# Two transformer layers on one core: the last MLP chunk gets a structure of its own

## The chip, the core and the metric

The kernel runs on one core of a Trainium2 chip. The metric is device time in microseconds (us) from launch to end. Five engines work in parallel, each through its own instruction stream in order: PE (TensorE, matrix products; PEld is its weight load), DVE (VectorE), ACT (ScalarE), POOL (GpSimd) and SP (SyncE, which issues most of the DMAs here). They meet only through semaphores.

## The reference

The input x has 2048 tokens of 640 bf16 values. Two layers are applied, each of them an attention part A and an MLP part B ("the mixer"), with one shared set of weights:

```
x = x + A(layernorm(x));  x = x + B(layernorm(x));  x = x + A(layernorm(x));  x = x + B(layernorm(x))

A: for each of 64 segments of 32 tokens, one after the other:
     h = [8 memory tokens, 32 tokens]                 # 40 rows
     q, k, v = h Wq, h Wk, h Wv                       # 640 -> 32 heads x 192
     o = softmax(mask(q k^T / sqrt(192))) v Wo        # -> 640
     memory of the next segment = the first 8 rows of o; output = the other 32
B: h  = gelu(layernorm(x) w1)                         # 640 -> 640
   hs = (h, its four quarters of columns moved by +1, -1, +2, -2 tokens) w2
   x1 = x + hs
   y  = x1 + gelu(layernorm(x1) w3) w4                # 640 -> 1536 -> 640
```

## The kernel before

A runs as 69 steps of `attention_step`. Step t handles segment t of the first layer (lane 0) and segment t - 5 of the second layer (lane 1) side by side, so that its matrix products have 80 columns; in the first five and in the last five steps only one lane is alive and they have 40. A step walks over 8 groups of 4 heads. `proj_pair` makes the projections for two groups (L541; results leave PSUM at L551, L559, L565 and L571, and `v` is transposed at L579), and `attend` makes scores, softmax and the output projection (L606 to L670, sum in `psy`). Most of the weights don't fit in SBUF: they are streamed again in every step through a ring of 8 slots (`wst`, L453).

B runs in chunks of 64 tokens per lane. `chunk` and `chunk_end` of number c are spread over the attention steps that follow, as filling for PE. A normal chunk does this, in order: transposes of the attention output back to rows (`psx`, L836), the residual sum (L847), layer norm statistics (`ln_ops`: two BN_STATS at L707, aggregation at L708, then variance + eps as two columns at L713 and L715, and the power -1/2 for both on POOL at L721), the normalised rows (L727), transposes (`psv`, L735), a copy of the result to SBUF by ACT (L896), w1 (`psh`, L918), `gelu` (ACT square L752, DVE L756, ACT tanh L760, DVE L765), w2 (`hs`, L963), the sum at L969, a second layer norm, transposes, copy (L983), w3 (L998), gelu, w4 (`y`, L1024), the sum at L1030 and the stores (L1042). Because w2 needs tokens beyond the chunk, a look-ahead is carried along for four rows: transposes `psl` (L843), a sum (L851), statistics (L874 to L876, POOL at L881), normalised rows (L887), which are written to the same buffer `vbg` as those of L727, a second set of transposes and a second copy (L900). After a normal chunk a third layer norm makes the input of the second layer's attention (`psn`).

The last chunk, `chunk(NCH - 1)`, has no attention step left to hide in. It starts when the last step's output is in `yTB` (L696), and everything in it follows in series. Its tokens are the last 34 and the last 64 before them. After the gelu of w1, seven small copies (`fc2`, L947) join its two lanes. Its w2, w3 and w4 are cut by the arrival of the weight loads, not by columns.

At the start, buffers are cleared by POOL (L373, L376, L380) and DVE ahead of everything else in their queues; POOL then issues three loads and computes the power of the first layer norm (L721), on which the first rows for attention wait (L727). Meanwhile SP loads the weights.

No order is written by hand. Each operation is given an estimated duration and a due time; `Plan.place` simulates the engines with these and fixes the order of all instructions before the program is built. A load that the plan holds back (`paced`) gets a wait on the PE operation that ends last before its planned start. A change of an estimated duration can thus move instructions elsewhere.

Of the kernel before, what the change touches and what calls it, by code (L numbers as in the profile page):

```python
# [29 lines left out]
OT_BUFS = 8  # L30
LAT = 0.12
# [44 lines left out]
class Plan:  # L76
# [47 lines left out]
    def place(self):  # L124
# [27 lines left out]
        def est(o, t):  # L152
            s = max(t, o.ready)
            need = {}
            for b in o.slots:
                if b.slot is None:
                    need[b.cls] = need.get(b.cls, 0) + 1
            for c, n in need.items():
                fs = self.free_slots[c]
                if len(fs) < n:  # L160
                    return None
                s = max(s, fs[n - 1][0])
            if o.e == "SP":
                s = max(s, srv - ahead(o))
            return s
# [6 lines left out]
        while left:  # L172
# [29 lines left out]
            o.paced = e == "SP" and s <= srv - ahead(o) + 1e-9  # L202
# [38 lines left out]
def kernel(  # L241
# [87 lines left out]
    mask_b = ctile([L1, L1], bf16, "mask_b")  # L329
    nc.gpsimd.memset(mask_b[:], 0.0)  # L330
    keep(mask_b, L1, M, L1, -M, 1, -1, NEG)
    keep(mask_b, L1, M, L1, -M, 1, 0, 0.0)
# [11 lines left out]
    qT = qTw[:].rearrange("p (c n) -> p c n", c=GC)  # L344
    vFw = ctile([P, GC * NS], bf16, "vF")
    vF = vFw[:].rearrange("p (c n) -> p c n", c=GC)
    kT = [ctile([P, 8, NS], bf16, f"kT{i}") for i in range(2)]
    Vt = [ctile([NS, 2 * VP], bf16, f"V{i}") for i in range(2)]
# [23 lines left out]
    for i in range(2):  # L372
        nc.gpsimd.memset(kT[i][:], 0.0)  # L373
    for i in range(2):
        nc.vector.memset(Vt[i][:], 0.0)
    nc.gpsimd.memset(yTB[:], 0.0)  # L376
    nc.vector.memset(qTw[:], 0.0)
    nc.vector.memset(vFw[:], 0.0)
    nc.vector.memset(Pmw[:], 0.0)
# [131 lines left out]
    def attention_step(t):  # L511
# [4 lines left out]
        maskt = mask2[:] if both else (mask_a if 0 in ln else mask_b[:])  # L516
# [8 lines left out]
        def proj_pair(pr):  # L525
            s0 = base + sl * 2 * pr
            for kind, off in (("k", 0.0), ("q", 0.2), ("v", 0.5)):
                wbs, wv = load_pair(kind, pr, s0 + off * 2 * sl, LEAD_A)
                for j in range(2):
                    g = 2 * pr + j  # L530
                    G = t * NG + g
                    due = s0 + (off + 0.1 * j) * 2 * sl
# [3 lines left out]
                    for kcs in [range(0, nres)] + [range(kc, kc + 1) for kc in range(nres, KC)]:  # L536
                        def fn(op, pq=pq, wv=wv, j=j, kcs=kcs):
                            o = T(pq)
                            for cc in range(GC):
                                for kc in kcs:  # L540
                                    nc.tensor.matmul(out=o[:, cc, 0:N],  # L541
                                                     lhsT=wv(kc, GW * j + cc * P, GW * j + (cc + 1) * P),
                                                     rhs=h[:, kc, c0:c0 + N], start=(kc == 0 and cc == 0),
                                                     stop=(kc == KC - 1), skip_group_check=True)
                        wb = wbs[0] if kcs[0] == 0 else wbs[1 + kcs[0] - nres]
                        add("PE", mm_us(N, k=GC * len(kcs)), due + 0.01 * kcs[0], fn, r=(wb, *hk), a=(pq,))
                    if kind == "q":
                        q = qT

                        def fq(op, pq=pq, q=q):  # L550
                            nc.scalar.copy(out=q[:, :, 0:N], in_=T(pq)[:, :, 0:N])  # L551
                        add("ACT", act_us(GC * N), due, fq, r=(pq,), w=(B("qT"),))
                    elif kind == "k":
                        k_ = kT[G % 2]

                        def fk(op, pq=pq, k_=k_):
                            p4 = T(pq)[:].rearrange("p (h c) n -> p h c n", h=2)
                            k4 = k_[:].rearrange("p (h c) n -> p h c n", h=2)
                            nc.vector.tensor_copy(out=k4[:, :, 0::3, 0:N], in_=p4[:, :, 0::2, 0:N])  # L559
                        add("DVE", dve_us(4 * N), due, fk, r=(pq,), w=(B("kT", G % 2, 0),))  # L560
                        for part, (r0, r1, jj) in enumerate(((0, 64, 1), (64, P, 2))):
                            def fk2(op, pq=pq, k_=k_, r0=r0, r1=r1, jj=jj):
                                p4 = T(pq)[:].rearrange("p (h c) n -> p h c n", h=2)
                                k4 = k_[:].rearrange("p (h c) n -> p h c n", h=2)
                                nc.vector.tensor_copy(out=k4[r0:r1, :, jj, 0:N], in_=p4[r0:r1, :, 1, 0:N])  # L565
                            add("DVE", dve_us(2 * N), due, fk2, r=(pq,), w=(B("kT", G % 2, 1 + part),))
                    else:
                        vf, V_ = vF, Vt[G % 2]

                        def fvf(op, pq=pq, vf=vf):  # L570
                            nc.scalar.copy(out=vf[:, :, 0:N], in_=T(pq)[:, :, 0:N])  # L571
# [3 lines left out]
                        def fvt(op, pvt=pvt, vf=vf):  # L575
# [6 lines left out]
                        for hf in range(2):  # L582
                            def fe(op, pvt=pvt, V_=V_, hf=hf):
                                src = T(pvt)[0:N, GWH * hf:GWH * (hf + 1)].rearrange("n (a b) -> n a b", a=2)
                                v0 = hf * (VP - 64)
                                dst = V_[0:N, v0:v0 + 512].rearrange("n (a b) -> n a b", a=2)[:, :, 64 * hf:64 * hf + Dh]
# [5 lines left out]
                                w=(B("V", G % 2, hf),))  # L592

        def attend(g):
            G = t * NG + g
            s0 = base + sl * g
            q, k_, V_ = qT, kT[G % 2], Vt[G % 2]
# [3 lines left out]
            def fs(op):  # L601
                o = T(pss)
                seq = [(0, 1, 0, 0), (1, 1, 2, 3), (2, 1, 3, 4), (3, 1, 5, 7), (0, 2, 1, 1), (2, 2, 4, 5)]
                for n_, (i, w_, c, j) in enumerate(seq):
                    m_ = wide(c, GC - 1)
                    nc.tensor.matmul(out=o[0:m_, i * N:(i + w_) * N].rearrange("p (a b) -> p a b", a=w_),  # L606
                                     lhsT=qTw[:, c * NS:c * NS + m_], rhs=k_[:, j:j + w_, 0:N],
                                     start=(n_ == 0), stop=(n_ == len(seq) - 1), skip_group_check=True)
            add("PE", mm_us(N, N, 4) + mm_us(2 * N, N, 2), hi - 4, fs,
                r=(B("qT"), B("kT", G % 2, 0), B("kT", G % 2, 1), B("kT", G % 2, 2)), w=(pss,))  # L610
# [4 lines left out]
            def f1(op):  # L615
                o = T(pss)[0:N, 0:HG * N].rearrange("p (a b) -> p a b", a=HG)
                nc.vector.tensor_tensor_reduce(out=o, in0=o, in1=maskt.unsqueeze(1).to_broadcast([N, HG, N]),  # L617
                                               scale=-scale, scalar=3.0e38, op0=ALU.add, op1=ALU.min,
                                               accum_out=sm_[0:N, 0:1])
            add("DVE", dve_us(HG * N) + 0.02, hi - 4, f1, r=(pss,), w=(pss, smk))  # L620

            def f2(op):
                o = T(pss)[0:N, 0:HG * N].rearrange("p (a b) -> p a b", a=HG)
                nc.scalar.activation(out=Pb[0:N, :, 0:N], in_=o, func=ACT.Exp, bias=sm_[0:N, 0:1], scale=-1.0)  # L624
            add("ACT", act_us(HG * N) + 0.09, hi - 4, f2, r=(pss, smk), w=(Pk,))

            def f3(op):
                nc.vector.tensor_reduce(out=sm_[0:N, 2:2 + HG], in_=Pb[0:N, :, 0:N], axis=AX.X, op=ALU.add)  # L628
                nc.vector.reciprocal(out=sm_[0:N, 6:6 + HG], in_=sm_[0:N, 2:2 + HG])
                nc.vector.tensor_tensor(out=Pb[0:N, :, 0:N], in0=Pb[0:N, :, 0:N],  # L630
                                        in1=sm_[0:N, 6:6 + HG].unsqueeze(2).to_broadcast([N, HG, N]), op=ALU.mult)
# [11 lines left out]
            def f5(op):  # L643
                nc.scalar.copy(out=Pt[:, :, 0:N], in_=T(pst)[0:NS, :, 0:N])  # L644
# [10 lines left out]
            add("PE", mm_us(N, k=8), hi - 3, f6, r=(B("PT"), B("V", G % 2, 0), B("V", G % 2, 1)), w=(pso,))  # L655
            o_ = oT[G % OT_BUFS]

            def f7(op):
                nc.vector.tensor_copy(out=o_[:, :, 0:N], in_=T(pso)[:, :, 0:N])  # L659
            add("DVE", dve_us(GC * N), hi - 4, f7, r=(pso,), w=(B("oT", G % OT_BUFS),))  # L660
            due = base + STEP - 1 + 0.02 * g if g >= NG - OT_BUFS + 1 else s0 + 2.0 * sl
            wb, wo = res_tile(("o", g), [P, GC, Dm], Wo_v[:, g], base + STEP - 2 + 0.02 * g)
            for hf in range(2):
                def f8(op, hf=hf):
                    o = T(psy)
                    for cc in range(3 * hf, 3 * hf + 3):
                        for m in range(KC):
                            st = first_wo[0]
                            first_wo[0] = False
                            nc.tensor.matmul(out=o[:, m, c0:c0 + N], lhsT=wo[:, cc, m * P:(m + 1) * P],  # L670
                                             rhs=o_[:, cc, 0:N], start=st, stop=True, skip_group_check=True)
                add("PE", mm_us(N, k=3 * KC), due, f8, r=(wb, B("oT", G % OT_BUFS)), a=(psy,))

# [26 lines left out]
    def ln_ops(src, rows, st, stk, srck, due, const_cols):  # L700
# [4 lines left out]
        def f1(op):  # L705
            for c in range(2):
                nc.vector.bn_stats(out=st[0:rows, 6 * c:6 * c + 6], in_=srcv[:, c, :])  # L707
            nc.vector.bn_aggr(out=st[0:rows, 12:14], in_=st[0:rows, 0:12].rearrange("p (c s) -> p c s", c=2))  # L708
            if const_cols:
                nc.vector.tensor_scalar(out=st[0:rows, 14:15], in0=st[0:rows, 13:14], scalar1=lnA[0:rows, 0:1],  # L710
                                        scalar2=lnA[0:rows, 1:2], op0=ALU.mult, op1=ALU.add)
            else:
                nc.vector.tensor_scalar(out=st[0:rows, 14:15], in0=st[0:rows, 13:14], scalar1=1.0, scalar2=EPS,  # L713
                                        op0=ALU.mult, op1=ALU.add)
                nc.vector.tensor_scalar(out=st[0:rows, 15:16], in0=st[0:rows, 13:14], scalar1=1.0 + EPS,  # L715
                                        scalar2=EPS * EPS, op0=ALU.mult, op1=ALU.add)
        add("DVE", 1.37, due, f1, r=(srck,), w=(stk,))
        n = 1 if const_cols else 2
# [106 lines left out]
    def chunk(c):  # L825
# [12 lines left out]
        psl = ps(PB, [TOK + 4, KC, P], bf16, "psl")  # L838
# [5 lines left out]
        add("PE", mm_us(128, k=KC), D(0.06), ftl, r=(B("yTB", 0), B("yTB", 1)), w=(psl,))  # L844
# [8 lines left out]
        add("DVE", 0.48, D(0.06), fl, r=(psl,), w=(B("lnx", "l"),))  # L853
# [13 lines left out]
        ln_ops(xw, XB, st1, s1k, xk, D(0.06), False)  # L867
# [10 lines left out]
        add("DVE", 1.42, D(0.07), f1, r=(B("lnx", "l"), B("lnx", "x")), w=(s2k,))  # L878
# [3 lines left out]
        add("POOL", 0.57, D(0.07), f2, w=(s2k,))  # L882
# [6 lines left out]
        add("DVE", 0.45, D(0.08), f3, r=(B("lnx", "l"), B("lnx", "x"), s2k), w=(vxk,))  # L889
        ps2 = ps(PB, [P, KC, XB], bf16, "psv")  # L890
        transposes(ps2, vb, XB, D(0.1), (vk,))
        psl2 = ps(PB, [P, KC, TOK + 4], bf16, "psvl")
        transposes(psl2, vx, TOK + 4, D(0.11), (vxk,))
# [3 lines left out]
        add("ACT", act_us(KC * XB), D(0.1), fe, r=(ps2,), w=(vTk,))  # L897
# [3 lines left out]
        add("ACT", act_us(KC * 4), D(0.11), fel, r=(psl2,), w=(B("vTl"),))  # L901
# [8 lines left out]
        for i, (a, e) in enumerate(((0, 2), (2, 4), (4, KC))):  # L910
# [10 lines left out]
            add("PE", mm_us(128, k=KC * (e - a)), due, fw, r=(wb, vTk, B("vTl")), a=tuple(pz))  # L921
# [5 lines left out]
        for i, (a, e) in enumerate(((0, 3), (3, KC))):  # L927
# [13 lines left out]
            gelu(pz[i], e - a, due, outs, (B("hTB", i),), own=i if last else None)  # L941
            carry += [(r, r1, n + a, o2) for (r, r1, n, _, _), o2 in zip(outs, offs)]
        if last:
            def fc2(op):
                for r, r1, n, o2 in carry:
                    if o2:
                        nc.vector.tensor_copy(out=hTB[r:r1, n, 0:o2 // 2, 0], in_=hTB[r:r1, n, TOK:TOK + o2 // 2, 1])  # L947
            add("DVE", 1.16, D(0.4), fc2, w=(B("hTB", 0), B("hTB", 1)))
# [4 lines left out]
        hs = [ps(PB, [XB, HC], f32, "hs") for _ in range(2)]  # L953
        for i, (a, e) in enumerate(((0, 2), (2, 4), (4, 5))):
            due = D(0.4 + 0.1 * i)
            wb, wv = load_b("w2", a, e, due, last=last)

# [7 lines left out]
            add("PE", mm_us(HC, k=2 * (e - a)), due, fw, r=(wb, B("hTB", 0), B("hTB", 1)), a=tuple(hs))  # L965
        for k in range(2):
# [194 lines left out]
```

## Time and profile before

| | |
|---|---|
| time, median of 3 runs | 3534.4 us (3530.97 to 3536.71) |
| the profiled execution | 3528.87 us, its span 3527.2 us |
| busy in the span | PE 94%, DVE 70%, ACT 43%, POOL 7% |
| last attention product (L670) ends | 3483.4 us |
| first product of the last chunk's w1, w2, w3 | 3491.04, 3498.50, 3506.30 us |
| last store is issued | 3517.18 us |

The span is the time from the first to the last instruction in one profiled execution; its own time is 1.7 us more. All positions are in us from the start of that span. In lists of instructions the columns are start, duration, engine, line, operation, output<-input, shapes, count and, in brackets, the idle time of the engine before it with what ended it. In tables by stretch PEclk is the clock that TensorE was granted, 1.00 being full speed.

### The profile page before, as it was taken

Reading aid. Unit: us, or ns where it says so; the run is one execution under the profiler, and the core shown is the slowest. Engines: PE = TensorE matmul, PEld = TensorE weight load, DVE = VectorE, ACT = ScalarE, POOL = GpSimd, SP = SyncE. Lnnn points to the kernel's source line nnn. Section 1 sums busy time; section 2 is a strip of 40 time slices with the busy share of each in tenths; the row PEclk is TensorE's granted clock in tenths of the full one; section 3 lists DMA queues with packets and bytes.
Section 4 is the critical chain, followed back from the end, with each engine's and each line's share of the span. In section 5 each row is a group of like instructions: output and inputs, shape, how many; then the busy total and the mean of one; then the engine's idle time right before and its main releaser. Section 6 shows DMA issues by size and latency. Waiting matters only on the chain.

```text
span 3527.2 us, 188048 instructions
## 1 busy us (share of the span) xinstructions
PE 3322.3 (94%) x84559; PEld 3231.6 (92%) x84559; DVE 2469.2 (70%) x7436; ACT 1520.6 (43%) x3569; POOL 247.1 (7%) x488
## 2 busy tenths in 40 slices
PE   5889999999999999999999999999999999999886
PEld 5879999999999999999999999999999999999775
DVE  2557777777777777777777777777777777777554
ACT  1334444444444444444444444444444444444332
POOL 0000000000000000000000000000000000000000
PEclk8899999999999999999999999999999999999897
DMA  9999898889888988898889888998889888988995
GB/s 374 304 306 317 301 324 298 294 297 316 301 307 299 315 300 299 309 321 303 302 301 327 306 295 298 316 310 303 312 305 319 298 299 301 319 300 303 307 315 176
DMA packets 497753, 1075.27 MB, mean 305 GB/s; under 512 B 49455, under 2 KB 216893, under 8 KB 496945
## 3 DMA queue, kind: packets, MB, share of 16 engines
q1 hardware_dynamic: 489712, 1050.11, 86.2%
q8 instruction: 661, 10.83, 1.2%
q0 software_dynamic: 7232, 13.13, 1.1%
q14 instruction: 148, 1.20, 0.1%
HBM read 1057.79 MB, written 5.24 MB: 301 GB/s over the span
## 4 chain that ended last, share of the span: by engine, by line
PE 88%; DMA 5%; issue 4%; DVE 1%; ACT 1%; SPq 1%; POOL 0%; POOLq 0%; DVEq 0%; ACTq 0%
PE psy L670 16%; PE psq L541 15%; PE psv L541 15%; PE psk L541 15%; PE pvt L579 5%; PE pso L653 4%; PE pss L606 4%; PE psh L998 3%; PE y L1024 3%; PE pst L639 2%; DMA wst<-in_A_Wq_dram 2%; PE psh L918 1%; DMA wst<-in_A_Wk_dram 1%; PE hs L963 1%; DMA wst<-in_A_Wv_dram 1%
## 5 line engine op out<-in xcount | busy, mean ns | idle before, releaser
L541 PEld LDWEIGHTS <-wst 128*128 128x128 bf16 x25668 | 1031.2, 100 | 43.1 <-issue 25.0
L670 PE MATMUL psy<-oT,wo 128*128 128x80 bf16 (+1 forms) x16560 | 689.8, 199 | 32.1 <-issue 19.4
L670 PEld LDWEIGHTS <-wo 128*128 128x128 bf16 x16560 | 626.3, 100 | 41.0 <-issue 29.2
L551 ACT CAST qT<-psq 128x480 bf16<-128x480 f32 (+1 forms) x552 | 292.6, 530 | 639.9 <-PE psq L541 638.6
L541 PE MATMUL psq<-hT,wst 128*128 128x80 bf16 (+1 forms) x9936 | 467.9, 199 | 19.1 <-issue 11.1
L659 DVE CAST oT<-pso 128x480 bf16<-128x480 f32 (+1 forms) x552 | 341.2, 618 | 167.2 <-PE pso L653 161.6
L541 PE MATMUL psv<-hT,wv 128*128 128x80 bf16 (+1 forms) x9936 | 434.6, 199 | 21.1 <-issue 15.9
L541 PE MATMUL psk<-hT,wst 128*128 128x80 bf16 (+1 forms) x9108 | 428.0, 199 | 11.0 <-issue 7.9
L541 PEld LDWEIGHTS <-wv 128*128 128x128 bf16 x9936 | 386.6, 100 | 28.9 <-issue 18.3
L644 ACT COPY PT<-pst 80x320 bf16<-80x320 bf16 (+1 forms) x552 | 221.9, 402 | 440.2 <-PE pst L639 433.8
L590 ACT COPY V<-pvt 80x384 bf16<-80x384 bf16 (+1 forms) x552 | 261.7, 474 | 328.5 <-PE pvt L579 301.1
L541 PE MATMUL psk<-hT,wk 128*128 128x80 bf16 (+1 forms) x7452 | 348.8, 199 | 19.5 <-ACT hT L688 10.8
L565 DVE CAST kT<-psk 64x160 bf16<-64x160 f32 (+1 forms) x1104 | 336.7, 305 | 9.7
L624 ACT ACTIVATE Pm<-pss,sm 80x320 bf16<-80x320 f32 (+1 forms) x552 | 279.7, 507 | 135.9 <-DVE sm L617 135.8
L571 ACT CAST vF<-psv 128x480 bf16<-128x480 f32 (+1 forms) x552 | 290.0, 525 | 102.0 <-PE psv L541 95.7
L541 PE MATMUL psq<-hT,wq 128*128 128x80 bf16 (+1 forms) x6624 | 320.2, 199 | 11.7 <-issue 6.6
L541 PE MATMUL psv<-hT,wst 128*128 128x80 bf16 (+1 forms) x6624 | 322.4, 199 | 7.7 <-issue 6.6
L541 PEld LDWEIGHTS <-wk 128*128 128x128 bf16 x7452 | 299.2, 100 | 26.8 <-issue 26.1
L588 DVE COPY V<-pvt 80x384 bf16<-80x384 bf16 (+1 forms) x552 | 188.1, 350 | 182.3 <-PE pvt L579 107.8
L617 DVE CUSTOM_DVE_ANT_1 pss<-pss,mask 80x320 f32<-80x320 f32 (+1 forms) x512 | 240.9, 485 | 104.7 <-PE pss L606 84.3
L559 DVE CAST kT<-psk 128x320 bf16<-128x320 f32 (+1 forms) x552 | 254.6, 461 | 69.6 <-PE psk L541 63.2
L628 DVE TENSOR_REDUCE sm<-Pm 80x4 f32<-80x320 bf16 (+1 forms) x552 | 248.9, 451 | 57.3 <-ACT Pm L624 52.2
(130 smaller groups left out, 4425.0 us busy)
## 6 DMA issues: line engine op xcount, KB each, us to landing
wst<-in_A_Wq_dram SPq DMA_DIRECT2D x828, 384.0 KB, 5.3
wst<-in_A_Wk_dram SPq DMA_DIRECT2D x759, 384.0 KB, 5.3
wst<-in_A_Wv_dram SPq DMA_DIRECT2D x552, 384.0 KB, 5.4
wstB<-in_B_w_dram SPq DMA_DIRECT2D x495, 320.0 KB, 5.0
wstB<-in_B_w_dram SPq DMA_DIRECT2D x132, 160.0 KB, 4.9
wo<-in_A_Wo_dram SPq DMA_DIRECT2D x8, 960.0 KB, 12.8
wv<-in_A_Wv_dram SPq DMA_DIRECT2D x4, 1152.0 KB, 11.9
wq<-in_A_Wq_dram SPq DMA_DIRECT2D x4, 768.0 KB, 11.7
```

The source lines that it names most:

```text
L541: nc.tensor.matmul(out=o[:, cc, 0:N], lhsT=wv(kc, GW * j + cc * P, GW * j + (cc + 1) * P), rhs=h[:, kc, c0:c0 + N], start=(kc == 0 and cc ...
L551: nc.scalar.copy(out=q[:, :, 0:N], in_=T(pq)[:, :, 0:N])
L559: nc.vector.tensor_copy(out=k4[:, :, 0::3, 0:N], in_=p4[:, :, 0::2, 0:N])
L565: nc.vector.tensor_copy(out=k4[r0:r1, :, jj, 0:N], in_=p4[r0:r1, :, 1, 0:N])
L571: nc.scalar.copy(out=vf[:, :, 0:N], in_=T(pq)[:, :, 0:N])
L590: nc.scalar.copy(out=dst, in_=src)
L617: nc.vector.tensor_tensor_reduce(out=o, in0=o, in1=maskt.unsqueeze(1).to_broadcast([N, HG, N]), scale=-scale, scalar=3.0e38, op0=ALU.add, ...
L624: nc.scalar.activation(out=Pb[0:N, :, 0:N], in_=o, func=ACT.Exp, bias=sm_[0:N, 0:1], scale=-1.0)
L628: nc.vector.tensor_reduce(out=sm_[0:N, 2:2 + HG], in_=Pb[0:N, :, 0:N], axis=AX.X, op=ALU.add)
L644: nc.scalar.copy(out=Pt[:, :, 0:N], in_=T(pst)[0:NS, :, 0:N])
L659: nc.vector.tensor_copy(out=o_[:, :, 0:N], in_=T(pso)[:, :, 0:N])
L670: nc.tensor.matmul(out=o[:, m, c0:c0 + N], lhsT=wo[:, cc, m * P:(m + 1) * P], rhs=o_[:, cc, 0:N], start=st, stop=True, skip_group_check=True)
```

## The change

In the last chunk:

- The look-ahead (`psl`, its sum, statistics, power, normalised rows, transposes, copy) is left out. The columns it filled are set to zero by a POOL memset or taken from the chunk's own transposes.
- The copy out of the transposes is cut in two, columns 0 to 2 by ACT and 3 to 4 by DVE (`halves`), for the first and for the second layer norm.
- Six of the seven small copies of `fc2` go from DVE to ACT.
- w2 and w4 are issued by halves of the output columns (k = 0, 1) within groups of row blocks, and each half has its sum (and, after w2, its BN_STATS) right behind it.
- w3 is issued as four groups of three row blocks, where it was three parts of 5, 5 and 2.
- The output is stored in four pieces, by row set and column half, issued by SP and ACT; it was two pieces issued by POOL.

Elsewhere:

- `ln_ops` makes one column of variance + eps where only one is used, which removes the DVE operation of L715 and halves the POOL power's columns in 68 layer norms; its planned duration falls from 1.37 to 1.30 us.
- In steps with lane 1 alone, operands stay at columns 40 to 79 instead of being moved to 0 to 39; the mask of their own (`mask_b`) goes. With `ONE = 40` their products keep 40 columns.
- At the start, eight buffers `oT` are cleared by POOL and four `hT` by DVE.
- Tiles are allocated in another order, `oT` is tracked by halves (`HALVES` is empty, so it is still written in one piece), and `paced` is set where the DMA rate alone delays a load.

```diff
-    mask_b = ctile([L1, L1], bf16, "mask_b")
-    nc.gpsimd.memset(mask_b[:], 0.0)
-    keep(mask_b, L1, M, L1, -M, 1, -1, NEG)
-    keep(mask_b, L1, M, L1, -M, 1, 0, 0.0)
+    mask_b = mask2[:, L1:NS]
...
+    for o_ in oT:
+        nc.gpsimd.memset(o_[:], 0.0)
...
+    for i in range(4):
+        nc.vector.memset(hT[i][:], 0.0)
...
-    def ln_ops(src, rows, st, stk, srck, due, const_cols):
+    def ln_ops(src, rows, st, stk, srck, due, n, parted=False):
...
-            for c in range(2):
+            for c in () if parted else range(2):
                 nc.vector.bn_stats(out=st[0:rows, 6 * c:6 * c + 6], in_=srcv[:, c, :])
...
+            if n == 2:
                 nc.vector.tensor_scalar(out=st[0:rows, 15:16], in0=st[0:rows, 13:14], scalar1=1.0 + EPS,
                                         scalar2=EPS * EPS, op0=ALU.mult, op1=ALU.add)
-        add("DVE", 1.37, due, f1, r=(srck,), w=(stk,))
-        n = 1 if const_cols else 2
+        add("DVE", (0.5 if parted else 1.3) + 0.07 * (n - 1), due, f1, r=(srck,), w=(stk,))
...
+        def halves(pt, due, ahead=False):
+            def fa(op):
+                nc.scalar.copy(out=vT[:, 0:3, 0:XB], in_=T(pt)[:, 0:3, :])
+            add("ACT", act_us(3 * XB), due, fa, r=(pt,), w=(vTk,))
+
+            def fd(op):
+                nc.vector.tensor_copy(out=vT[:, 3:KC, 0:XB], in_=T(pt)[:, 3:KC, :])
+            add("DVE", dve_us(2 * XB), due, fd, r=(pt,), w=(B("vTd"),))
+            if ahead:
+                def fn(op):
+                    nc.scalar.copy(out=vT[:, :, XB + 1:XB + 4:2], in_=T(pt)[:, :, 0:4:2])
+                add("ACT", act_us(KC * 2), due, fn, r=(pt,), w=(B("vTn"),))
...
+        if last:
+            def fz0(op):
+                nc.gpsimd.memset(vT[:, :, XB:XB + 4:2], 0.0)
+            add("POOL", 0.3, D(0.02), fz0, w=(vTk,))
+            halves(ps2, D(0.1), True)
...
         if last:
-            def fc2(op):
-                for r, r1, n, o2 in carry:
-                    if o2:
-                        nc.vector.tensor_copy(out=hTB[r:r1, n, 0:o2 // 2, 0], in_=hTB[r:r1, n, TOK:TOK + o2 // 2, 1])
-            add("DVE", 1.16, D(0.4), fc2, w=(B("hTB", 0), B("hTB", 1)))
+            for i in range(2):
+                mine = [x for x in carry if x[3] and (x[2] < 3) == (i == 0)]
+                for e_, part in (("ACT", mine if i == 0 else []), ("DVE", [] if i == 0 else mine)):
...
+        for u, (n0, n1) in enumerate(((0, 3), (3, 5))) if last else ():
+            for k in range(2):
+                def fw(op, k=k, n0=n0, n1=n1):
+                    for n in range(n0, n1):
+                        lhsT = hTB[:, n, 0:TOK, :].rearrange("p w l -> p (w l)")
+                        nc.tensor.matmul(out=T(hs[k])[:], lhsT=lhsT, rhs=got[n][1]()[:, got[n][2], HC * k:HC * (k + 1)],
+                                         start=(n == 0), stop=(n == 4))
...
+                if last:
+                    nc.vector.bn_stats(out=st3[:, 6 * k:6 * k + 6], in_=uw[:, cs])
...
+        for u in range(4) if last else ():
+            n0 = 3 * u
+            pz2 = ps(PB, [P, 3, XB], f32, "psh2")
+
+            def fw(op, n0=n0, pz2=pz2):
+                for kc in range(KC):
+                    for n in range(n0, n0 + 3):
+                        _, wv, j, i = w3got[n, kc]
+                        nc.tensor.matmul(out=T(pz2)[:, n - n0, :], lhsT=wv()[:, j, i * P:(i + 1) * P],
+                                         rhs=vT[:, kc, 0:XB], start=(kc == 0 and n == n0), stop=(kc == KC - 1),
+                                         skip_group_check=True)
...
+        for u, (n0, n1) in enumerate(((0, 3), (3, 6), (6, 9), (9, FC))) if last else ():
+            for k in range(2):
+                def fw(op, k=k, n0=n0, n1=n1):
+                    for n in range(n0, n1):
+                        nc.tensor.matmul(out=T(y2[k])[:], lhsT=h2T[:, n, :], rhs=got[n][1]()[:, got[n][2], HC * k:HC * (k + 1)],
+                                         start=(n == 0), stop=(n == FC - 1))
...
+                def fst(op, lane=lane, b=b, w0=w0, cs=slice(HC * k, HC * (k + 1))):
+                    (nc.scalar if lane else nc.sync).dma_start(out=outd[w0:w0 + b, cs], in_=xo[lane:2 * b:2, cs])
+                add("ACT" if lane else "SP", 0.4, D(1.6), fst, r=(B("xh", k),), dma=b * HC * 2)
```

## The prediction

> **What bounds the kernel now.** The page first: who is busy, and the chain that ended last.
>
> ```profile
> PE 3322.3 (94%) x84559; PEld 3231.6 (92%) x84559; DVE 2469.2 (70%) x7436; ACT 1520.6 (43%) x3569; POOL 247.1 (7%) x488
> PE   5889999999999999999999999999999999999886
> PEclk8899999999999999999999999999999999999897
> PE 88%; DMA 5%; issue 4%; DVE 1%; ACT 1%; SPq 1%; POOL 0%; POOLq 0%; DVEq 0%; ACTq 0%
> ```
>
> PE is the bound nearly everywhere: 88% of the chain. What relieves DVE or POOL in the middle is worth little. The exception is the end, read next in stretches of 10 us.
>
> ```profile
> 3480.00:3490.00 10.00, 3.95 (x94) 3.38 (x93) 6.56 (x20) 0.76 (x2) 1.39 (x2) 0.83 1.02 335
> 3490.00:3500.00 10.00, 4.79 (x38) 3.75 (x37) 4.39 (x18) 2.36 (x6) 0.22 (x1) 0.50 0.07 24
> 3500.00:3510.00 10.00, 5.74 (x46) 4.71 (x45) 3.48 (x11) 1.46 (x3) 0.88 (x1) 0.50 0.01 2
> 3510.00:3520.00 10.00, 5.23 (x51) 3.80 (x49) 4.50 (x12) 3.08 (x8) 1.14 (x2) 0.98 0.04 13
> ```
>
> Here no engine is busy for more than two thirds (columns: PE, PEld, DVE, ACT, POOL), TensorE runs at half clock for most of it, and the DMA engines are empty: one chain of dependent steps. The timeline shows its links.
>
> ```profile
> 3484.95 0.49 DVE L851 TENSOR_TENSOR h2u<-psl,h2u 4x640 bf16<-4x640 bf16 x1
> ...
> 3488.97 0.44 DVE L887 TENSOR_SCALAR vbg<-h2u,st 68x640 bf16<-68x640 bf16 x1
> ...
> 3489.47 0.71 PE L735 MATMUL psv<-ident,vbg 128*128 128x128 bf16 x5 [4.79 <-DVE vbg L887]
> 3490.22 0.69 ACT L896 COPY hTB<-psv 128x640 bf16<-128x640 bf16 x1 [8.93 <-PE psv L735]
> 3490.80 0.18 ACT L900 COPY hTB<-psvl 128x20 bf16<-128x20 bf16 x1
> 3491.04 2.29 PE L918 MATMUL psh<-hTB,wk 128*128 128x128 bf16 x20 [0.57 <-ACT hTB L900]
> ...
> 3495.42 2.90 DVE L765 SCALAR_TENSOR_TENSOR hTB<-wv,psh 128x128 bf16<-128x128 f32 x9 [0.33 <-ACT wv L760]
> 3498.23 1.16 DVE L947 COPY hTB<-hTB 128x3 bf16<-128x3 bf16 x7
> ...
> 3501.09 0.89 DVE L969 SCALAR_TENSOR_TENSOR h2u<-hs,h2u 128x320 bf16<-128x320 f32 x2 [1.70 <-PE hs L963]
> ...
> 3516.60 1.14 POOL L1042 DMA_DIRECT2D out_dram<-vbg  x2 [12.37 <-DVE vbg L1030]
> ```
>
> The look-ahead sits on the chain: its sum (L851) stands ahead of the main statistics on DVE, and the main transposes wait for its normalised rows (L887), since both write `vbg`.
>
> **The change part by part.** The end, from the first `psx` transpose at 3483.95.
>
> *To the first w1 product: before 3491.04, so 7.09.* After, with these rows' durations and 0.03 to 0.05 per hand-over: `psx` 0.48, sum 0.49, two BN_STATS 0.89, aggregation 0.21, the two columns 0.21, which brings POOL's power to 2.46; 0.71 (it stays at two columns) to 3.17; normalised rows 0.44 to 3.64; `psv` 0.71 to 4.40. Then the halves. They are not parallel: in the built program DVE's copy waits on the ACT semaphore at the value that ACT's copy raises, and the small ACT copy waits for DVE's. So 0.48 (ACT, 384 columns; L590 takes 0.474 for as many) + 0.30 (DVE, 256; L588 takes 0.350 for 384) + 0.18 (L900) + hand-overs = 1.1, where L896 and L900 took 0.85. First w1 product at 5.5: **-1.6**. Parallel halves would make it -1.9. The POOL memset of the padding stands far ahead in POOL's queue and costs nothing.
>
> TensorE's clock decides the 0.71 and the w1 products. The row: PEclk was 0.80 over 3486 to 3487 and 0.50 from then on, so it fell 2.1 us after the last product at 3484.7. The Trainium skill ("TensorE: Matmul & The Clock Gate", "What's actually happening") says the clock halves after at least one idle window of about 3.4 us. The gap before `psv` shrinks to about 3.2 us, so by the page alone the clock could hold through `psv` and w1: 0.3 off the transposes and about 1.2 off the 25 w1 products (2.84 at half clock), 1.5 more gain. The trace shows the fall inside such a gap; I take half clock, and keep 1.5 for the range.
>
> *w1 to the first L765:* unchanged, 4.38.
>
> *L765 to the first w3 product: before 3495.42 to 3506.30, 10.88.* The nine L765 pieces keep 2.90. Six of the seven copies run on ACT, each behind its DVE piece, at about 0.2 (L900: 0.182); the sixth ends 2.0 after the start. Products of the first three row blocks begin at once after that: ten products of 320 columns took 2.83 here, 0.27 each at half clock. Left column half to 2.3, right one to 3.15; the last DVE copy (0.17) ends at 3.1; two products more for the left half, and its sum starts at 3.8, where before it was 5.67: -1.87. The right half's last products run beside it. Sum, BN_STATS, sum, BN_STATS, aggregation now alternate with waits between: 2.10, before 1.93, +0.17. One column less, -0.07. Power (0.88 beside L976), rows and transposes stay. w3 needs only ACT's 384 columns for its first nine products (0.107 apart), and DVE's part is ready by then: -0.21. Together **-2.0**; first w3 product at 18.8, before 22.35.
>
> *w3 to the last sum: before 3506.30 to 3516.31, 10.0.* The 60 products cost the same 5.5, half of them cold. After the fourth group ACT and DVE alternate in the planned order: square to 6.0, DVE 0.55 for each of the last three steps (L756 and L765 at 384 columns), tanh 0.52; the last L765 ends at 7.8. The third group's six w4 products end at 8.2, the last six at 9.0 (0.136 each at full clock), sums at 9.15 and 9.63: **-0.4**. With cold w4 products it would be +0.9.
>
> *Stores:* the last issue began 0.87 after the last sum, behind POOL's first; now 0.1 after, on a queue of its own: **-0.8**. From issue to landing both stores took 1.9. The memory load that SP issues at 1.27 on an idle queue is used at 3.17, 1.9 as well, so I take nothing more. The skill ("DMA: Bandwidth & Descriptors", "Specifications") gives first-byte times of about 1 us from GpSimd and 0.6 from SP or ACT, an estimate of -0.4 more.
>
> End: -1.6 - 2.0 - 0.4 - 0.8 = **-4.8**.
>
> *The start.* POOL clears eight `oT` of 480 columns ahead of its loads and of the first power; `kT` with 640 took 0.62, so 0.47 each, 3.7, less 0.5 for the mask. The power moves from 7.04 to about 10.3, and PE's first projections with it.
>
> ```profile
> 7.04 0.76 POOL L721 TENSOR_TENSOR st<-st,neghalf 128x2 f32<-128x2 f32 x1
> 7.84 0.45 DVE L727 TENSOR_SCALAR vbg<-vbg,st 128x640 bf16<-128x640 bf16 x1 [3.02 <-POOL st L721]
> ...
> 12.63 0.98 PE L541 MATMUL psq<-hT,wq 128*128 128x40 bf16 x24 [1.04 <-DMA wq<-in_A_Wq_dram]
> ...
> 19.40 1.38 PE L541 MATMUL psv<-hT,wv 128*128 128x40 bf16 x36 [1.80 <-DMA wv<-in_A_Wv_dram]
> ```
>
> But PE waits for weights at 12.63, twice at about 15 and at 19.40, 3.7 in all; that covers 3.2. SP's next load into a ring slot (12.67) may go 2 us late; loads then take 12.5 from issue to landing, a backlog that covers it. Cost 0; bounds 0 and +3.2. DVE's four `hT` memsets (under 0.26 each, the price of `qT`) end long before the power.
>
> *The middle.* 68 DVE operations go, 0.07 apart behind L713. On the chain such a one appears at few places, as here:
>
> ```profile
> 1722.19 0.06 DVE st L715
> ```
>
> Five in the whole trace: **-0.3**; if every one told, -4.7. The shorter planned duration reorders little: of 10,097 PE groups 180 stand elsewhere (steps 2 to 5, 65, 67). Of 2,492 held-back loads 216 wait for another PE group, mostly one later. PE's queue, the loads' sizes and the 40-column products are unchanged. Bounds -4.7 and +10 (see the last rival); taken -0.3.
>
> **Sum:** -5.1 on the profiled 3528.87, so 3523.8. The median of the runs stands 5.5 higher, at 3534.4; from there 3529.3.
>
> **The rivals.** *A second gain* (0.35): PE keeps its clock at the end, or DVE's relief reaches PE in the middle. -5.1 with 1.5 and 0.4 at the end, or 2.3 to 4.7 in the middle: -7.5 to -12, 3522 to 3527. For it: the ordered DVE queue puts softmax pieces behind each layer norm, 67 times. Against: the chain meets that five times. *The start is not covered* (0.05): +3.2, net -1.9, 3532.5. Against: the waits above. *The loads come later* (0.10): from step 6 on, four to five of some 76 held-back loads of every two steps wait for a PE group more, 0.15 to 0.65 us. PE's idle time put to "issue", 4% of the chain in pieces of 1 to 2 us, could be late weights. If one of them per chunk delays PE by 0.4, 32 chunks cost 12.8, net +7.7, 3542. It decides from 0.16 per chunk, where the end's gain is used up. Against: a ring of eight slots lies between.
>
> **How the numbers follow.** A measurement of this kernel tells about 0.2%, 7.1 us, from no change. The forecast (0.50) has its own range 3526 to 3532; 0.08 of it lies past -7.1. Faster: 0.08 + 0.35 = 0.43; same: 0.42 + 0.05 = 0.47; slower 0.10. Range 3520 to 3537: it takes in the second gain but its far end, and the uncovered start, and leaves out the late loads.
>
> **What would show it.** Right: no L851 to L887 counterparts after the last step; first w1 product 5.5 after `psx`, first w3 product 18.8, last store issue about 28.6 (before 33.2); the two half copies one after the other; PEclk at 0.50 before w1; PE's first projection near 12.7 but `psv` still at 19.4; the last attention product within 2 us of 3483.4. Wrong: that product moved by more than 3 us either way, or `psv` at the start later by more than 1.

## The result and the profile after

The changed kernel takes 3513.57 us (median of 6 runs, 3508.64 to 3526.6), the kernel before 3535.56 us (6 runs, 3530.97 to 3538.52). The ratio is 0.9946, with a 95% interval of 0.9926 to 0.9966: 19 us faster, between 12 and 26. The forecast was 5 us faster (3529.3 us, range 3520 to 3537), less than the 7 us that it took as the least a measurement can tell from no change.

The profiled execution of the changed kernel is its slowest run, 3526.6 us (span 3524.9), only 2.3 below that of before. So the two traces must be compared by stages. The sum of the span hides that the attention part happened to run late in this execution and that the end is far shorter. First the page, then stretches of the end (PE, PEld, DVE, ACT, POOL busy; PEclk; DMA share; GB/s).

```profile
PE 3321.0 (94%) x84549; PEld 3229.3 (92%) x84549; DVE 2466.7 (70%) x7360; ACT 1522.1 (43%) x3573; POOL 235.7 (7%) x489
PE 90%; issue 4%; DMA 3%; DVE 1%; ACT 1%; SPq 0%; POOL 0%; POOLq 0%; DVEq 0%; ACTq 0%
```

```profile
3500.00:3510.00 10.00, 4.67 (x24) 2.42 (x22) 6.08 (x19) 2.75 (x10) 0.91 (x2) 0.50 0.00 0
3510.00:3520.00 10.00, 8.76 (x89) 7.07 (x89) 4.97 (x11) 4.11 (x9) 0.03 (x1) 0.79 0.01 2
3520.00:3525.00 5.00, 0.20 (x2) 0.00 (x0) 0.73 (x2) 0.00 (x0) 0.00 (x0) 0.94 0.09 25
```

Nothing is won in busy time. The last attention output (L716, L696 of before) starts at 3492.28, where before it was 3483.46, and yet the span ends 2.3 earlier. From that output to the end of the span it was 43.7 and is 32.6: **11.1 us less**. The links of that chain, from the timeline of the changed kernel:

```profile
3493.51 0.49 DVE L864 TENSOR_TENSOR xw<-psx,xw 128x640 bf16<-128x640 bf16 x1 [0.88 <-PE psx L852]
3494.03 0.89 DVE L727 BATCH_NORM_STATS2 st<-xw 128x6 f32<-128x320 bf16 x2
...
3496.75 0.72 PE L751 MATMUL psv<-ident,vbg 128*128 128x128 bf16 x5 [3.29 <-DVE vbg L743]
...
3497.51 0.48 ACT L919 COPY hTB<-psv 128x384 bf16<-128x384 bf16 x1 [7.68 <-PE psv L751]
3498.02 0.29 DVE L923 COPY hTB<-psv 128x256 bf16<-128x256 bf16 x1 [0.96 <-ACT hTB L919]
3498.40 0.18 ACT L927 COPY hTB<-psv 128x10 bf16<-128x10 bf16 x1 [0.41 <-DVE hTB L923]
3498.63 2.29 PE L959 MATMUL psh<-hTB,wk 128*128 128x128 bf16 x20 [1.16 <-ACT hTB L927]
...
3503.02 2.69 DVE L781 SCALAR_TENSOR_TENSOR hTB<-wv,psh 128x128 bf16<-128x128 f32 x9 [0.33 <-ACT wv L776]
3503.34 1.65 ACT L992 COPY hTB<-hTB 128x3 bf16<-128x3 bf16 x6
...
3506.86 0.49 DVE L1032 SCALAR_TENSOR_TENSOR h2u<-hs,h2u 128x320 bf16<-128x320 f32 x1 [1.08 <-PE hs L1024]
...
3511.91 0.80 PE L1089 MATMUL psh<-hTB,wv 128*128 128x128 bf16 x6 [0.62 <-ACT hTB L919]
...
3519.84 0.90 DVE L1133 SCALAR_TENSOR_TENSOR vbg<-y,xw 128x320 bf16<-128x320 f32 x2 [0.81 <-PE y L1125]
3520.36 1.20 ACTq L1145 DMA_DIRECT2D out_dram<-vbg  x2
3520.39 1.39 SPq L1145 DMA_DIRECT2D out_dram<-vbg  x2
```

The look-ahead is gone: BN_STATS follows the sum, and the transposes wait for the main rows. The two half copies stand one behind the other. The small copies run on ACT beside DVE's pieces. Cut at the marks that the prediction used, the end reads as follows in all six kernels profiled (E1 to E4 are the experiments below; us):

| stretch | before | E3 | E4 | changed | E1 | E2 |
|---|---|---|---|---|---|---|
| `psx` to the first w1 product | 7.09 | 7.35 | 7.34 | 5.85 | 5.85 | 5.85 |
| w1 to the first gelu piece (L765) | 4.38 | 4.39 | 4.39 | 4.39 | 4.39 | 4.38 |
| gelu piece to the first w3 product | 10.88 | 10.46 | 10.62 | 8.89 | 8.89 | 8.90 |
| w3 to the end of the last sum | 10.01 | 9.73 | 9.73 | 8.83 | 9.73 | 8.93 |
| end of the last sum to the end of the span | 10.89 | 10.82 | 4.69 | 4.16 | 10.77 | 4.33 |

The first four rows bring 1.2, 0, 2.0 and 1.2 us. The last one brings 6.7, more than all others together, in a stretch where no engine computes. What SP waits for there tells where the time goes (columns: waiting engine and line, what it waited for: total us, times, longest). Before:

```profile
SPq L1156 <- DMA out_dram<-vbg: 29.1, 1, 29.1
SPq L1156 <- PEq L1156: 7.7, 2, 7.2
```

and in the changed kernel:

```profile
SPq L1271 <- DMA out_dram<-vbg: 1.6, 2, 1.0
SPq L1271 <- PEq L1271: 0.7, 2, 0.5
```

At the end of the program SP first waits until every DMA has landed, and then meets the other engines. Before, the stores had landed by 3519.1 and the meeting still took 7.2 us; now it takes 0.5. The wait is put down to PE's queue, but PE came early: its closing DRAIN (the instruction with which each engine ends its work before the meeting) was over at 3515.6. The engine that came last was POOL. These are POOL's DRAINs in before, the changed kernel, E1 and E4 (line, engine, operation, count: least, median and longest in ns, first and last start in us):

```profile
L1156 POOLq DRAIN  x3: 46/102/9346, 3517.0 to 3526.9; - x3
L1271 POOLq DRAIN  x3: 46/93/9174, 3509.3 to 3524.6; - x3
L1271 POOLq DRAIN  x3: 46/98/9259, 3514.3 to 3524.0; - x3
L1157 POOLq DRAIN  x3: 46/102/9411, 3507.5 to 3524.4; - x3
```

The first of the three is the long one. It takes 9.2 to 9.4 us in every kernel; what differs is when POOL comes to it (its record begins up to 0.9 us before POOL's last operation ends):

| | before | E1 | E3 | E4 | changed | E2 |
|---|---|---|---|---|---|---|
| POOL's last operation | store | store | store | power | power | power |
| it ends | 3517.74 | 3514.96 | 3525.91 | 3508.46 | 3510.03 | 3502.07 |
| POOL's long DRAIN ends | 3526.38 | 3523.52 | 3534.55 | 3516.96 | 3518.45 | 3510.48 |
| SP is ready for the meeting | 3519.41 | 3516.49 | 3527.53 | 3523.95 | 3524.11 | 3516.43 |

In all six the DRAIN ends 8.4 to 8.6 us after POOL's last operation, be that a store or the power of the second layer norm. With the stores on POOL the others wait 7.0 us for it. Without them it runs beside the last chunk's arithmetic and is over 5.7 to 7.0 us before SP is ready.

### The profile page after: what moved, and what is told of

The parts are those of the page before. It is cut to its first block, busy times and chain, and to the rows that moved or that the text cites. A ratio compares the mean times of both kernels' runs of the same rounds, so it can differ in the third digit from the quotient of the medians.

```text
span 3524.9 us, 187932 instructions
## 1 busy us (share of the span) xinstructions
PE 3321.0 (94%) x84549; PEld 3229.3 (92%) x84549; DVE 2466.7 (70%) x7360; ACT 1522.1 (43%) x3573; POOL 235.7 (7%) x489
## 4 chain that ended last, share of the span: by engine, by line
PE 90%; issue 4%; DMA 3%; DVE 1%; ACT 1%; SPq 0%; POOL 0%; POOLq 0%; DVEq 0%; ACTq 0%
PE psy L690 16%; PE psk L551 16%; PE psq L551 16%; PE psv L551 15%; PE pvt L589 5%; PE pso L663 4%; PE pss L616 4%; PE psh L1073 3%; PE y L1118 3%; PE pst L649 2%; DMA wst<-in_A_Wk_dram 2%; PE psh L959 1%; PE hs L1015 1%; PE psv L751 1%; DMA wst<-in_A_Wv_dram 1%
## 5 line engine op out<-in xcount | busy, mean ns | idle before, releaser
L551 PE MATMUL psq<-hT,wst 128*128 128x80 bf16 (+1 forms) x9936 | 466.6, 199 | 10.9 <-issue 7.9
L551 PE MATMUL psk<-hT,wst 128*128 128x80 bf16 (+1 forms) x9108 | 427.2, 199 | 11.1 <-issue 8.8
L600 ACT COPY V<-pvt 80x384 bf16<-80x384 bf16 x552 | 262.0, 475 | 342.0 <-PE pvt L589 311.7
L551 PE MATMUL psk<-hT,wk 128*128 128x80 bf16 (+1 forms) x7452 | 349.1, 199 | 20.0 <-ACT hT L708 11.1
L627 DVE CUSTOM_DVE_ANT_1 pss<-pss,mask 80x320 f32<-80x320 f32 (+2 forms) x552 | 253.9, 474 | 140.5 <-PE pss L616 130.6
L634 ACT ACTIVATE Pm<-pss,sm 80x320 bf16<-80x320 f32 (+2 forms) x552 | 279.9, 507 | 136.9 <-DVE sm L627 136.6
L598 DVE COPY V<-pvt 80x384 bf16<-80x384 bf16 x552 | 188.6, 350 | 175.8 <-PE pvt L589 96.8
L589 PE MATMUL pvt<-ident,vF 128*128 128x128 bf16 x3312 | 282.8, 222 | 11.7 <-issue 8.8
```

The source lines that it names most:

```text
L551: nc.tensor.matmul(out=o[:, cc, 0:W], lhsT=wv(kc, GW * j + cc * P, GW * j + (cc + 1) * P), rhs=h[:, kc, cw:cw + W], start=(kc == 0 and cc ...
L589: nc.tensor.transpose(out=o[0:w_, c * P:(c + 1) * P], in_=vFw[:, c * NS:c * NS + w_], identity=ident[:, :])
L600: nc.scalar.copy(out=dst, in_=src)
L634: nc.scalar.activation(out=Pb[0:NR, :, c0:c0 + N], in_=o, func=ACT.Exp, bias=sm_[0:NR, 0:1], scale=-1.0)
```

## The experiments

**E1: the stores back on POOL.** Everything else is the changed kernel.

```diff
-            for lane in range(2) if last else ():
...
-                    (nc.scalar if lane else nc.sync).dma_start(out=outd[w0:w0 + b, cs], in_=xo[lane:2 * b:2, cs])
-                add("ACT" if lane else "SP", 0.4, D(1.6), fst, r=(B("xh", k),), dma=b * HC * 2)
+        for lane in range(2) if last else ():
...
+                nc.gpsimd.dma_start(out=outd[w0:w0 + b, :], in_=xo[lane:2 * b:2, :])
+            add("POOL", 0.9, D(1.55), fst, r=(B("xh", 0), B("xh", 1)), dma=b * Dm * 2)
```

> The changed kernel, with its last stores given back to POOL: two row sets, whole rows, behind both sums. Theory (the end of the program pays about 6 us for two stores that POOL issues last): the stretch from the last sum's end to the end of the span goes from 4.2 us back to about 10.9 us, and the time rises by 6 to 7 us over the changed kernel. Rival (the stores are worth only what their issue took, 0.8 us, and the rest of the end is noise): the stretch grows by 1 us at most.

Measured: 3524.37 us against 3537.73 of before, ratio 0.9960 (0.9945 to 0.9976); by the ratios some 5 us above the changed kernel, with intervals that overlap. The trace decides: 10.77 us from the last sum to the end, and the long meeting is back, with POOL's DRAIN at its end. SP's waits in E1:

```profile
SPq L1271 <- DMA out_dram<-vbg: 28.7, 2, 28.5
SPq L1271 <- PEq L1271: 7.7, 2, 7.2
```

The rival, that only the issue is worth something, is out.

**E4: the kernel before, with only its two last stores moved.**

```diff
-                nc.gpsimd.dma_start(out=dst[w0 + a:w0 + b, :], in_=xo[2 * a + lane:2 * b:2, :])
-            add("POOL", 0.9,
+                eng = (nc.scalar if lane else nc.sync) if last else nc.gpsimd
+                eng.dma_start(out=dst[w0 + a:w0 + b, :], in_=xo[2 * a + lane:2 * b:2, :])
+            add(("ACT" if lane else "SP") if last else "POOL", 0.9,
```

> The kernel before with only its two last stores moved from POOL to SP and ACT, whole rows. Theory (stores from POOL cost about 6 us at the end of the program): 6 to 7 us faster than before, the stretch from the last sum's end to the span's end 10.9 to about 4.5 us. Rival (only the issue): 1 us faster, stretch about 10 us.

Measured: 3528.98 against 3537.73 us, ratio 0.9976 (0.9963 to 0.9988), 8.5 us faster with an interval of 4 to 13. The stretch is 4.69 us. The last lines of E4's timeline and SP's waits:

```profile
3519.12 0.89 DVE L1030 SCALAR_TENSOR_TENSOR vbg<-y,xw 128x320 bf16<-128x320 f32 x2 [1.37 <-PE y L1024]
3520.04 0.56 ACTq L1043 DMA_DIRECT2D out_dram<-vbg  x1
3520.09 0.70 SPq L1043 DMA_DIRECT2D out_dram<-vbg  x1
```

```profile
SPq L1157 <- DMA out_dram<-vbg: 2.1, 1, 2.1
SPq L1157 <- PEq L1157: 0.7, 2, 0.5
```

With whole rows and two stores, one edit of three lines has nearly all of the 6.7; the other 0.5 (4.69 to 4.16) goes with the cut into column halves. E1 and E4 change the same thing in opposite directions in two kernels, and both move that stretch by 6.2 to 6.6.

**E2: the changed kernel with the layer norm of before,** work and planned duration, except in the last chunk's second one. The planned order of the attention part is then that of before but for one pair.

```diff
-            if n == 2:
+            if not parted:
                 nc.vector.tensor_scalar(out=st[0:rows, 15:16], in0=st[0:rows, 13:14], scalar1=1.0 + EPS,
...
-        add("DVE", (0.5 if parted else 1.3) + 0.07 * (n - 1), due, f1, r=(srck,), w=(stk,))
+        add("DVE", 0.5 if parted else 1.37, due, f1, r=(srck,), w=(stk,))
+        n = 1 if parted else 2
```

> The changed kernel, with the layer norm's second column and its planned duration of 1.37 us put back everywhere but in the last chunk's second layer norm; the planned order of the attention part is then that of before but for one pair. Theory (the shorter layer norm, by its DVE work or by the new order and the later held-back loads, brings the 11 us that the end does not explain): the time rises by about 11 us over the changed kernel, to some 11 us below before. Rival (the 11 us come from another part of the change: start, operands in place, tile addresses): it stays within 3 us of the changed kernel.

Measured: 3520.98 against 3537.73 us, ratio 0.9950 (0.9930 to 0.9970), where the changed kernel has 0.9946. The theory asked for a loss of 11 us (0.3%); the ratio moved by 0.04%, or 1 us. That speaks against the theory, but the intervals of both kernels together leave room for 11 us; E3 decides.

**E3: the kernel before with the short layer norm alone,** so with the new order and the new waits of the held-back loads.

```diff
-                nc.vector.tensor_scalar(out=st[0:rows, 15:16], in0=st[0:rows, 13:14], scalar1=1.0 + EPS,
-                                        scalar2=EPS * EPS, op0=ALU.mult, op1=ALU.add)
-        add("DVE", 1.37, due, f1, r=(srck,), w=(stk,))
-        n = 1 if const_cols else 2
+                if src is xw:
+                    nc.vector.tensor_scalar(out=st[0:rows, 15:16], in0=st[0:rows, 13:14], scalar1=1.0 + EPS,
+                                            scalar2=EPS * EPS, op0=ALU.mult, op1=ALU.add)
+        n = 2 if src is xw else 1
+        add("DVE", 1.3 + 0.07 * (n - 1), due, f1, r=(srck,), w=(stk,))
```

> The kernel before with the short layer norm alone, work and planned duration, so with the new order and the new waits of the held-back loads. Theory (layer norm brings the middle's gain): about 11 us faster than before. Rival (another part): within 3 us of before.

Measured: 3541.13 against 3537.73 us, ratio 1.0001 (0.9985 to 1.0017). Neither the theory's gain of 11 us nor the prediction's last rival, late loads at +12.8, is in it: the interval goes from -5 to +6. The theory falls. The 67 layer norms in the middle, the new order and the later loads, as far as they come from the shorter planned duration, are together worth nothing that can be measured.

**What stays open.** The end explains 11.1 of 19 us. The other 8 (between 1 and 15, by the interval) are not explained. The comparison of the runs with the traces leaves a rest in each kernel that has the other parts of the change, and none in those that have not:

| | by the ratio, us | by the trace of the end, us | rest, us |
|---|---|---|---|
| changed | -19 (-26 to -12) | -11.1 | -8 |
| E2 | -18 (-25 to -11) | -10.9 | -7 |
| E1 | -14 (-19 to -8) | -3.6 | -11 |
| E4 | -8.5 (-13 to -4) | -6.5 | -2 |
| E3 | 0 (-5 to +6) | -0.5 | +1 |

Parts that E1, E2 and the changed kernel share and the others lack are the start, the operands left in place in the steps with lane 1 alone, the tile addresses, the new rule for `paced` and the last chunk. Single traces don't show the rest: the last attention output came at 3483.5, 3492.1 and 3487.4 in before, E3 and E4, and at 3492.3, 3484.2 and 3484.3 in the changed kernel, E1 and E2; the means, 3487.7 and 3486.9, differ by 0.8. One stage looks different: steps 64 to 67, which have lane 1 alone, take 195.9, 196.5 and 194.6 in the first three and 192.5, 193.5 and 191.7 in the others, about 3 less. But the step after that has lane 1 alone too and gives back some 1.3, and over all five the two groups overlap (237.7, 240.4, 236.9 against 238.1, 236.4, 235.3). The memory copies at the end of steps 63 and 67 (L688, L708), before and then changed:

```profile
3245.76 0.19 ACT L688 CAST hT<-psy 128x40 bf16<-128x40 f32 x1 [2.74 <-PE psy L670]
...
3441.64 0.19 ACT L688 CAST hT<-psy 128x40 bf16<-128x40 f32 x1 [2.67 <-PE psy L670]
```

```profile
3254.24 0.19 ACT L708 CAST hT<-psy 128x40 bf16<-128x40 f32 x1 [2.74 <-PE psy L690]
...
3446.78 0.19 ACT L708 CAST hT<-psy 128x40 bf16<-128x40 f32 x1 [2.34 <-PE psy L690]
```

So at most 2 of the 7 to 11 may lie there, and three traces of each kind don't show even that. A kernel with everything but the last chunk, which would tell scatter from a gain in the middle, was not run, nor was one that moves only the tiles. So the cause of the rest is not settled.

## Why the prediction was wrong, step by step

- **The stores, the step that failed.** The term was -0.8 and measured -6.7 (E4 alone: -6.2). It was worked out from the issues, and everything behind the landing was carried over unchanged as if every kernel had it. The issues came as forecast: the last one 28.4 after the first `psx` transpose, with 28.6 forecast. But the earlier issue brought nothing by itself. From the end of the last sum until all was landed it took 2.7 us before and 2.9 in the changed kernel, because SP's last store needed 2.5 from issue to landing, not the 1.9 that was carried over. What the prediction left out is the step after that: in the trace of before the last store has landed at 3519.05, and the span ends at 3527.2. These 8 us could be seen in it; 7.0 of them were the wait for POOL's DRAIN, which the move of the stores took off the end. The further 0.4 that was estimated from the Trainium skill ("DMA: Bandwidth & Descriptors", "Specifications"), which gives SP and ACT a shorter first-byte time than GpSimd, doesn't show either: for the same two stores, from issue to landing, it took 1.9 on ACT and 2.9 on SP in E4, and 1.9 each on POOL in before.
- **How much of the miss that is.** The forecast was 5 us and the result 19. The stores are 5.9 of the difference of 14, and the other terms of the end together 0.4. The remaining 8 or so are the rest above, for which the prediction had -0.3, and their cause is open. With the stores' term right, and nothing else, the forecast would have been about 3523 us, 10 above the measured median.
- **w3 to the last sum:** -0.4 forecast, -1.2 measured, but the size is partly chance. The clock came back 2.3 us after the start of w3 in the changed kernel and 4.2 before. PEclk is the third figure from the end; first before, then changed:

```profile
3510.00:3511.00 1.00, 1.00 (x16) 1.00 (x15) 0.74 (x3) 0.83 (x2) 0.00 (x0) 0.75 0.00 0
```

```profile
3513.00:3514.00 1.00, 1.00 (x13) 1.00 (x11) 0.00 (x0) 0.30 (x1) 0.00 (x0) 0.50 0.06 16
3514.00:3515.00 1.00, 1.00 (x19) 1.00 (x18) 0.55 (x1) 0.34 (x2) 0.00 (x0) 0.90 0.00 0
```

  So like must be compared with like. Where it came back late, the new code took 9.73 (E1, after 4.6) and the old 10.01 (before, after 4.2). Where it came back early, the new took 8.83 and 8.93 (changed and E2, after 2.3 and 2.5) and the old 9.73 (E3 and E4, after 2.9 and 2.7). The new structure of w3 and w4 is thus worth 0.3 to 0.9, and the rest of the 1.2 is the clock.
- **Look-ahead and half copies:** 5.85 against a forecast of 5.5, a gain of 1.2 where 1.6 was forecast. In this run `psx` itself was at half clock (0.69 instead of 0.44); against E3 and E4, where it was too, the gain is 1.5. The copies stood in series, as forecast, at 0.48, 0.29 and 0.18. The clock was at 0.50 through `psv` and w1 in the changed kernel, E1 and E2, and the 1.5 us more did not come. But it had fallen before `psx` already, so these runs don't test whether it would have held through the shorter gap. That the half clock was right is in part luck.
- **L765 to w3:** -2.0 forecast, -2.0 measured; the sum after w2 starts 3.84 after the first piece (3.8 forecast). The mechanism was right too: `hs` products begin behind the first small copies on ACT.
- **The start:** right in cost. POOL clears `oT` for 3.6 us and the power moves to 10.20 (10.3 forecast); the projections that follow absorb it, and the first step's output is at 88.39 where it was 88.69.

```profile
3.81 3.13 POOL L379 MEMSET oT<- 128x480 bf16 x7
...
10.20 0.62 POOL L737 TENSOR_TENSOR st<-st,neghalf 128x1 f32<-128x1 f32 x1
...
14.44 0.97 PE L551 MATMUL psq<-hT,wq 128*128 128x40 bf16 x24
...
18.11 1.11 PE L551 MATMUL psv<-hT,wv 128*128 128x40 bf16 x36 [0.50 <-DMA wv<-in_A_Wv_dram]
```

  PE no longer waits for `wq`, since it comes later itself; `psv` is not later than before.
- **The middle:** -0.3 forecast for the layer norms; E3 and E2 agree with that and with zero. The rival of late loads falls with E3. The prediction's sign of being wrong, a last attention product moved by more than 3 us, came up (3492.25, 8.8 later), but proves nothing: E3 is as late with the short layer norm alone, and E1 and E2 are within 1 us of before. One trace of each can't tell that.
- **A reading:** "the DMA engines are empty" holds from 3490 on. In 3480 to 3490 its own row has them full (1.02, 335 GB/s), with the last chunk's weights.
- **The rivals:** "a second gain" came nearest in size, and neither reason that it named was found: the clock was not kept, and the layer norms brought nothing. A rest of 7 to 11 us in the middle may be real, and the forecast had nothing for it that the experiments confirm.

## What to carry to other kernels

Read the profile to the end of the span: the distance from the last landing to the end is a term of the sum. SP's waits show how long the last meeting takes, and the records of the program's closing line (here L1156) show which engine came last to it; the name in SP's wait was not that one. Where POOL works until the end of a program, as with the last store here, give that work to another engine, so that POOL's DRAIN runs beside the rest; here it was three lines for 6 us, more than all restructuring of the last chunk's arithmetic. And when runs scatter by 10 us, compare stages of the traces, not spans.

## What the runs showed of the hardware

- POOL's closing DRAIN took 9.17 to 9.41 us in all six kernels and ended 8.4 to 8.6 us after POOL's last operation. It isn't the price of a late store: in the changed kernel POOL's last DMA had moved its data by 3441.2, 68 us before the DRAIN began, and the DRAIN took 9.17 all the same. The closing DRAINs of PE, DVE and ACT took 1.5 us at most in before. All six kernels issue DMAs from POOL earlier in the program, so whether POOL's DRAIN would be short in a kernel that never does is not known.
- TensorE's clock went to half 1.9 us after the last product in before (at 3486.6, by the 0.80 over 3486 to 3487; the prediction has 2.1) and 0.3 after the last attention product in E1; in the changed kernel it was at half before the last attention products had ended. The idle window of about 3.4 us that the prediction cites doesn't fit E1, where PE was busy for 2.35 of the 3.41 us before the fall. The clock came back 2.3 to 4.6 us after the start of w3's continuous products. With the same instructions this moves a stretch of 9 us by 0.9.
